# Scores copied to SBUF by VectorE, and transpositions in row halves for two heads, in an attention and two-expert kernel

## The chip, the cores and the metric

The kernel runs on 1 core of one Trainium2 chip. The metric is the device time of one execution in microseconds (us); lower is better. The engines are named as the profile names them: PE is TensorE (PEld its weight loads), DVE is VectorE, ACT is ScalarE, POOL is GpSimd, SP is SyncE, which issues most DMAs.

## The reference

Attention over 2 batches and 8 heads (576 positions of 64), then two expert layers of 1152 x 512 x 2048 x 512, one with the Mish activation, one with a rational function:

```python
q_rot, k_rot = (rotate(q), rotate(k))
scores = scale * np.matmul(q_rot, k_rot.transpose(0, 1, 3, 2))
scores = scores - np.max(scores, axis=-1, keepdims=True)
attn = np.exp(scores)
attn = attn / (np.sum(attn, axis=-1, keepdims=True) + 1e-09)
attn_out = np.matmul(attn, v)
...
h = x @ w_in;  g = h * np.tanh(softplus(h));  x = g @ w_out
h = x @ w_in;  g = P(h) / (Q(h) + 1e-6);      out = g @ w_out
```

## The kernel before, in words

**The attention part** goes over 8 pairs of heads (`NPR`; 2 batches x 4). Of each pair the 576 queries are 4 tiles of 128 rows for each of the two heads, and a last tile (t = 4) that holds the remaining 64 rows of both. For a pair the program issues, each as an operation of a plan:

- `rope.1` to `rope.4` (POOL, for the first pair also DVE) rotate q and k; `turn` (L579, PE) transposes them tile by tile into one PSUM bank; `turn.hi` (L591, ACT) rounds the result, times 0.125 for q, to fp32r in SBUF, and `turn.lo` (L597, L599, DVE) stores what the rounding left.
- `score` (L626, PE): 12 matmuls for the two heads of a tile. Each head uses 64 rows of the array, so that the two can run beside each other; the last tile uses all 128 rows and 6 matmuls. A head's tile takes two of the eight PSUM banks.
- `score.max` (L640, DVE) reduces the scores to their negated maximum; `score.exp` (L644, ACT) reads the scores from PSUM and writes the exponentials to SBUF, with their sum.
- `p.turn` (PE): for a tile and one head four transpositions of 128 x 128 (L681) into one bank, and for two tiles together the rest columns; the last tile's ten transpositions are already halves of 64 rows (L672 to L675). `p.move` (L694, ACT) and `p.move2` (L698, DVE) take turns at copying the bank to SBUF.
- `weigh` (L727, PE) multiplies with v, in two column ranges (256 and 320); `weigh.move` (L732, ACT) copies the result.
- `sum.inv` (L747, L748, DVE) inverts the sums, `sum.turn` (L763, PE) transposes them, `sum.row` and `sum.lo` (L765 ACT, L767 DVE) split them, `sum.spread` (L753, L755, PE) spreads them over the partitions, `x.scale` (L760, DVE) multiplies; `x.hi` and `x.lo` (L771, L773, POOL) split the result.

**The expert part** has two layers, four chunks of 512 hidden columns each, three blocks of 384 tokens: `up` (L886) 48 matmuls, the activation on ACT and DVE, `down` (L970). Weights come as 64-bit words; `prepare` loads half a chunk (1 MB, L390) and rebuilds it with `w.size` (L404, ACT), `w.bound` (L419), `w.shift` (L422), `w.low` (L425) on DVE, `w.hi` (L435, ACT) and `w.lo` (L439, DVE). The four halves of the first chunk are prepared during the attention, through one buffer, so that each load waits until the half before it has been read; the second chunk's buffers lie over memory of the attention.

**What sets the order.** `Plan.op` only records an operation with a cost; `Plan.emit` places them by a list schedule. It takes the operation that could start first (plus a `YIELD` for its name), ties by rank, which is the place in the program plus `EARLY_LATE` for its name; a change of an operation's `form` on PE (all 128 rows, halves of rows, halves of columns) costs 95 ns there, and PSUM banks are given out in the same pass. So each engine's queue is a fixed list that the plan wrote, and each engine works it off in order.

Of the kernel before, what the change touches and what calls it, by code (L numbers as in the profile page):

```python
# [7 lines left out]
F32 = mybir.dt.float32  # L8
# [36 lines left out]
def pool(n, wide=False):  # L45
# [13 lines left out]
    "down": 6381, "down.0": 651, "down.add": -4660, "down.add.0": -371, "g.hi": -1666, "g.hi.0": 8818, "g.lo":  # L59
    2324, "g.low": -4168, "g.low.0": -2960, "load": -4036, "mish": -591, "mish.0": 818, "p.move": -5661,  # L60
    "p.move2": -499, "p.turn": -2139, "ratio.1": 3382, "ratio.10": -1773, "ratio.11": -229, "ratio.2": -62,
    "ratio.3": 1635, "ratio.4": -866, "ratio.5": -3076, "ratio.6": -9113, "ratio.7": -2268, "ratio.9": 3319,
    "rope.1": 6275, "rope.3": 3669, "score": 36, "score.exp": -2880, "start": 868, "store": -567, "sum.inv": 4264,
    "sum.lo": -1016, "sum.row": 11927, "sum.spread": 164, "sum.turn": -1062, "turn": -2960, "turn.hi": 4495,
    "turn.lo": 3138, "up": 645, "up.0": -548, "w.bound": 596, "w.bound.0": 530, "w.hi": 478, "w.hi.0": -4430,
    "w.keep": 262, "w.lo.0": -2459, "w.load": 7247, "w.load.0": 427, "w.low": 168, "w.low.0": 321, "w.shift":
    -187, "w.shift.0": 1322, "w.size": 9168, "w.size.0": 129, "weigh": -325, "weigh.move": 200, "x.hi": -2880,
    "y.hi": -2684, "y.lo": 5352}
# [4 lines left out]
    "down.add": 555, "g.hi": 2, "g.hi.0": 640, "g.lo": 641, "g.low.0": 400, "mish": 1313, "mish.0": 616, "p.move":  # L73
    207, "p.move2": 534, "p.turn": 269, "ratio.10": 67, "ratio.5": 52, "ratio.6": 18, "ratio.8": 170, "ratio.9":
    475, "rope.1": 270, "score.exp": 125, "score.max": 433, "start": 205, "store": 572, "sum.inv": 814, "turn":
    321, "turn.lo": 638, "up.0": 1444, "w.bound": 72, "w.bound.0": 568, "w.hi": 116, "w.hi.0": 287, "w.keep":
    1276, "w.lo": 54, "w.lo.0": 1414, "w.load": 2261, "w.load.0": 559, "w.low.0": 702, "w.shift": 143,
    "w.shift.0": 471, "w.size": 690, "w.size.0": 1181, "weigh": 545, "weigh.move": 548, "x.scale": 189, "y.hi":
    160}
# [177 lines left out]
def block_kernel(ctx: ExitStack, tc: tile.TileContext, q, k, v, w1_in, w1_out, w2_in, w2_out,  # L257
# [205 lines left out]
    ROPE_T = ("tab",)  # L463
# [61 lines left out]
    def turned_first(x, b1, b2, engine):  # L525
# [16 lines left out]
    def turned(p, n, engine, ts=slice(0, 5), at=None):  # L542
# [14 lines left out]
        plan.op("rope.1", engine, cost(128 * m), lambda: eng.tensor_tensor(m1, t4, c, ALU.mult), r=[*src, ROPE_T], w=k1)  # L557
        plan.op("rope.2", engine, cost(128 * m), lambda: eng.tensor_tensor(m2, t4, s, ALU.mult), r=[*src, ROPE_T], w=k2)
# [5 lines left out]
    def columns(p, u, ts=slice(0, 4)):  # L564


        P = Banks(1)
# [9 lines left out]
        def pe():  # L577
            for n, (x, i) in enumerate(rows):
                nc.tensor.transpose(bank(P)[:, n * 128:(n + 1) * 128], view(x.off + 128 * i, 128), idf)  # L579

        def moves():
            x = bank(P)
            if u == "q":
                return [(qT[:, :, c], x[:, 0:m], 0.125)]
            if u == "k":
                return [(kT[:, :, c], x[:, 0:m], 1.0)]
            return [(qT[:, :, 512:640], x[:, 0:128], 0.125)] * (u == "e") + [(kT[:, :, 512:S], x[:, m - 64:m], 1.0)]

        def hi():
            for o, i, f in moves():  # L590
                nc.scalar.mul(o[:, 0], i, f)  # L591

        def lo():
            for o, i, f in moves():
                h = o[:, 0].bitcast(F32)
                if f == 1.0:
                    nc.vector.tensor_tensor(o[:, 1], i, h, ALU.subtract)  # L597
                else:
                    nc.vector.scalar_tensor_tensor(o[:, 1], i, f, h, ALU.mult, ALU.subtract)  # L599
# [6 lines left out]
        plan.op("turn", "PE", 110 * len(rows), pe, r=src + [("idf",)], w=[(P,)])  # L606
# [3 lines left out]
    def score(p, t):  # L610
# [19 lines left out]
        plan.op("score", "PE", 6 * 130 + 15, pe, r=src, w=[(P,) for P in Ps], form="rows" if t < 4 else "all")  # L630
# [25 lines left out]
    def turn_p(p, a, t):  # L656

# [411 lines left out]
```

## Time and profile before

| | |
|---|---|
| time before, median of 3 runs | 561.43 us (561.18 to 561.87) |
| profiled execution: span from first to last instruction | 559.8 us |
| the profiled execution's own time | not listed apart from its span; the runs' median lies 1.63 us above the span |
| busy: PE, DVE, ACT, POOL | 537.8, 453.3, 355.4, 95.8 us |
| attention on PE (first transposition pair to the closed run of `up`) | 10.15 to 161.80 us |
| experts on PE | 161.80 to 555.85 us |

A busy time is the union of an engine's instructions; the mean of one instruction holds a tail that the next one overlaps, so the pace of a queue is read from start to start in the timeline. Idle time is only worth something on the engine that the others wait for.

### The profile page before, as it was taken

What the parts mean: (1) busy time and instruction counts of PE and PEld (TensorE: products, weight loads), DVE (VectorE), ACT (ScalarE), POOL (GpSimd) and SP (SyncE); (2) the same over time, 40 slices, a digit from 0 to 9 for tenths busy, and PEclk for the clock granted to TensorE, in tenths of its full rate; (3) what the DMA queues carried; (4) which work ended last, traced back from release to release, by engine and by line L of the source; (5) the groups of instructions that cost most, each with busy time, mean ns of one, the idle gap of its engine ahead of it and who ended that gap; (6) DMA issues with size and microseconds to landing.
All of it is one profiled execution on the core that took longest, in us unless ns stands there. A gap on an engine that the chain in (4) does not pass through costs nothing.

```text
span 559.8 us, 8739 instructions
## 1 busy us (share of the span) xinstructions
PE 537.8 (96%) x3416; PEld 487.5 (87%) x3416; DVE 453.3 (81%) x618; ACT 355.4 (63%) x540; POOL 95.8 (17%) x100
## 2 busy tenths in 40 slices
PE   3999999999999999999999999999999999999997
PEld 2776777677699999999999999998999988899985
DVE  4777878898938798875999882869999999999982
ACT  1767676687748566837666845658476766776540
POOL 6989878211110000000000000000000000000000
PEclk9999999999999999999999999999999999999999
DMA  5253122311453958382879414044005301200012
GB/s 152 68 151 70 42 62 49 92 49 58 148 170 142 366 199 328 141 309 87 319 273 348 173 81 151 0 151 150 2 1 171 130 1 54 97 2 0 1 70 100
DMA packets 38681, 69.35 MB, mean 124 GB/s; under 512 B 22000, under 2 KB 24560, under 8 KB 37104
## 3 DMA queue, kind: packets, MB, share of 16 engines
q1 hardware_dynamic: 37824, 68.50, 35.2%
q8 instruction: 27, 0.44, 0.3%
q10 hardware_dynamic: 816, 0.30, 0.2%
q14 instruction: 14, 0.11, 0.1%
HBM read 53.84 MB, written 14.94 MB: 123 GB/s over the span
## 4 chain that ended last, share of the span: by engine, by line
PE 91%; DVE 4%; ACT 3%; DMA 1%; issue 1%; SPq 0%; ACTq 0%; DVEq 0%
PE banks L886 36%; PE banks L970 35%; PE banks L681 6%; PE banks L727 6%; PE banks L626 6%; ACT f L644 2%; DVE f L640 2%; PE banks L579 1%; PE banks L753 1%; DMA x<-in_k 1%; DVE f L747 1%; DVE f L422 0%; DVE f L531 0%; PE banks L755 0%; PE banks L672 0%
## 5 line engine op out<-in xcount | busy, mean ns | idle before, releaser
L886 PE MATMUL banks<-r 128*128 128x384 f32 x1152 | 203.7, 335 | 0.0
L970 PE MATMUL banks<-r 128*128 128x384 f32 (+1 forms) x1008 | 201.6, 358 | 0.0
L886 PEld LDWEIGHTS banks<-r 128*128 128x128 f32 x1152 | 200.3, 188 | 0.7
L970 PEld LDWEIGHTS banks<-r 128*128 128x128 f32 x1008 | 180.9, 188 | 16.5
L644 ACT ACTIVATE f<-banks,f 128x576 f32<-128x576 f32 x72 | 52.9, 741 | 23.4 <-DVE f L640 23.1
L640 DVE TENSOR_REDUCE f<-banks 128x1 f32<-128x576 f32 x72 | 51.2, 752 | 16.6 <-PE banks L626 15.9
L976 DVE TENSOR_TENSOR x<-banks,x 128x384 f32<-128x384 f32 (+1 forms) x63 | 35.9, 608 | 11.6 <-PE banks L970 11.6
L626 PE MATMUL banks<-r 64*128 64x288 f32 (+1 forms) x432 | 42.5, 315 | 0.5 <-ACT r L591 0.5
L681 PE MATMUL banks<-f 128*128 128x128 f32 x288 | 40.5, 281 | 2.0 <-ACT f L644 1.9
L727 PE MATMUL banks<-x,f 128*64 128x256 f32 (+1 forms) x320 | 42.4, 411 | 0.0
L912 DVE TENSOR_TENSOR r<-f,r 128x768 fp32r<-128x768 f32 x24 | 22.5, 954 | 24.0 <-ACT f L908 15.9
L626 PEld LDWEIGHTS banks<-r 64*128 64x128 f32 (+1 forms) x432 | 34.6, 192 | 7.0 <-issue 3.5
L681 PEld LDWEIGHTS banks<-f 128*128 128x128 f32 x288 | 32.0, 142 | 7.8 <-ACT f L644 3.9
L908 ACT ACTIVATE r<-banks 128x768 fp32r<-128x768 f32 x24 | 19.4, 813 | 30.2 <-PE banks L886 30.2
L934 ACT ACTIVATE f<-banks,f 128x768 f32<-128x768 f32 x24 | 23.4, 987 | 19.5 <-DVE r L897 14.1
L727 PEld LDWEIGHTS banks<-x,f 128*64 128x64 f32 x320 | 22.1, 136 | 14.5 <-issue 1.4
L938 ACT ACTIVATE f<-f 128x768 f32<-128x768 f32 x24 | 22.5, 938 | 15.2 <-DVE f L933 14.6
L936 DVE TENSOR_TENSOR f<-f,banks 128x768 f32<-128x768 f32 x24 | 22.7, 954 | 11.2 <-ACT f L928 7.0
L896 ACT CAST r<-f 128x768 fp32r<-128x768 f32 x24 | 19.9, 830 | 15.8 <-DVE f L944 15.6
L698 DVE COPY x<-banks 128x512 f32<-128x512 f32 (+2 forms) x52 | 28.6, 572 | 1.2 <-PE banks L681 0.9
L931 ACT ACTIVATE f<-f 128x768 f32<-128x768 f32 x24 | 24.7, 1029 | 6.0 <-DVE f L944 5.6
L694 ACT COPY x<-banks 128x512 f32<-128x512 f32 (+2 forms) x52 | 24.4, 500 | 2.8 <-PE banks L681 2.4
(83 smaller groups left out, 661.8 us busy)
## 6 DMA issues: line engine op xcount, KB each, us to landing
f<-in_moe_w_in SPq DMA_DIRECT2D x16, 1024.0 KB, 6.0
f<-in_moe_w_out SPq DMA_DIRECT2D x16, 1024.0 KB, 6.5
outside<-f SPq DMA_DIRECT2D x12, 1024.0 KB, 4.0
r<-outside SPq DMA_DIRECT2D x12, 1024.0 KB, 6.0
out<-x SPq DMA_DIRECT2D x8, 256.0 KB, 2.4
x<-in_k SPq DMA_DIRECT2D x15, 128.0 KB, 2.8
f<-in_q SPq DMA_DIRECT2D x8, 128.0 KB, 3.2
f<-in_v SPq DMA_DIRECT2D x8, 128.0 KB, 2.4
```

Source lines behind the costliest of these rows:

```text
L626: nc.tensor.matmul(bank(Ps[h])[:, hf, 0:HW], qT[r, x, t * 128:(t + 1) * 128], kT[r, y, hf * HW:(hf + 1) * HW], start=(n == 0), stop=(n == 2))
L640: nc.vector.tensor_reduce(nm, bank(P)[:, :, 0:HW], axis=AX.XY, op=ALU.max, negate=True)
L644: nc.scalar.activation(view(at, 2, HW), bank(P)[:, :, 0:HW], AF.Exp, bias=nm, accum_out=sm)
L681: nc.tensor.transpose(bank(P)[:, (i + n) * 128:(i + n + 1) * 128], x[:, f:f + 128], idf)
L694: nc.scalar.copy(o, i)
L698: nc.vector.tensor_copy(o, i)
L727: nc.tensor.matmul(bank(P)[64 * a:64 * a + 64, 0:n], l, r, start=(kb == 0), stop=(kb == 4), skip_group_check=True)
L886: nc.tensor.matmul(bank(P)[:, i, 0:BW], y[:, cb, f], x[:, cb, tok], start=(cb == 0 and n == 0), stop=(cb == CB - 1 and n == 2))
L931: plan.op("ratio.2", "ACT", act(N, False, 2), lambda: nc.scalar.activation(q_, a, AF.Identity, bias=prm[:, 4:5], scale=prm[:, 5:6]), r=[(b ...
L934: plan.op("ratio.4", "ACT", act(N, True, 2), lambda: nc.scalar.activation(t, h(), AF.Identity, bias=prm[:, 2:3], scale=prm[:, 3:4]), r=[(P ...
L970: nc.tensor.matmul(bank(P)[:, 0:n], x, y, start=(f == 0 and j == 0), stop=(f == FT - 1 and j == 2))
L976: nc.vector.tensor_tensor(total(), bank(P)[:, 0:n], total(), ALU.add)
```

## The change

VectorE no longer only reduces the scores. One instruction multiplies them by -0.125, writes them to SBUF, where the exponentials will stand, and keeps their minimum; the exponential reads SBUF, in place, with scale -1. The factor 0.125 leaves the q columns. The PSUM banks of a tile are free once VectorE is done. Transpositions of q, k, exponentials and sums are done as two halves of 64 rows, the halves in two banks; one `p.turn` does both heads of a tile (16 halves in place of 8 whole ones), and its two moves take one half each, of both heads. `sum.inv` writes its first step to PSUM. All plan costs around this, `EARLY_LATE` and `YIELD` are new, so the order is new on every engine.

```diff
-    return 200.0 if a == "PE" else 80.0 if a == "POOL" else 157.0 if b == "POOL" else 145.0 if a == "ACT" else 118.0
+    return 250.0 if a == "PE" else 80.0 if a == "POOL" else 157.0 if b == "POOL" else 145.0 if a == "ACT" else 118.0
...
+    HALVES = slice(0, 64), slice(64, 128)
...
-        P = Banks(1)
+        P = Banks(2)
...
-                nc.tensor.transpose(bank(P)[:, n * 128:(n + 1) * 128], view(x.off + 128 * i, 128), idf)
+                for hf, r in enumerate(HALVES[:1 if x is xk and i == 4 else 2]):
+                    nc.tensor.transpose(bank(P)[:, hf, n * 64:(n + 1) * 64], view(x.off + 128 * i, 128)[r], idf[r, r])
...
-        plan.op("turn", "PE", 110 * len(rows), pe, r=src + [("idf",)], w=[(P,)])
+        plan.op("turn", "PE", 60 * len(rows) + 20, pe, r=src + [("idf",)], w=[(P,)], form="rows")
...
-            nc.vector.tensor_reduce(nm, bank(P)[:, :, 0:HW], axis=AX.XY, op=ALU.max, negate=True)
+            nc.vector.tensor_scalar(view(at, 2, HW), bank(P)[:, :, 0:HW], -0.125, None, ALU.mult, ALU.min, accum_out=nm)
...
-            nc.scalar.activation(view(at, 2, HW), bank(P)[:, :, 0:HW], AF.Exp, bias=nm, accum_out=sm)
-
-        plan.op("score.max", "DVE", dve(576, True), most, r=[(P,)], w=[(T["nm", p], i)])
-        plan.op("score.exp", "ACT", act(576, True, 2), exp, r=[(P,), (T["nm", p], i)], w=[(e, h), (T["sm", p], i)], form="exp")
+            nc.scalar.activation(view(at, S), view(at, S), AF.Exp, bias=nm, scale=-1.0, accum_out=sm)
+
+        plan.op("score.max", "DVE", dve(576, True) + 90, most, r=[(P,)], w=[(T["nm", p], i), (e, h)])
+        plan.op("score.exp", "ACT", act(576, False, 2), exp, r=[(T["nm", p], i)], w=[(e, h), (T["sm", p], i)], form="exp")
...
-                k = [512] if a is None else [(S + 64) * a + kb * 128 for kb in range(4)]
+                k = [512] if what == "r" else [(S + 64) * a + kb * 128 for a in range(2) for kb in range(4)]
                 for n, f in enumerate(k):
-                    nc.tensor.transpose(bank(P)[:, (i + n) * 128:(i + n + 1) * 128], x[:, f:f + 128], idf)
...
+                    for hf, r in enumerate(HALVES):
+                        nc.tensor.transpose(bank(P)[:, hf, (i + n) * 64:(i + n + 1) * 64], x[r, f:f + 128], idf[r, r])
...
-            nc.vector.tensor_scalar_add(sm, sm, 1e-9)
-            nc.vector.reciprocal(sm, sm)
+            nc.vector.tensor_scalar_add(bank(P)[:, 0, 64:73], sm, 1e-9)
+            nc.vector.reciprocal(sm, bank(P)[:, 0, 64:73])
```

Where the queues stand otherwise than before, at the two places that matter most. First PE's queue in one of the later pairs (L626, after the change L628, is `score`; L681, then L683, `p.turn`; L727, then L732, `weigh`; L753 and L755, then L765 and L767, `sum.spread`). Before:

```order
L626 MATMUL banks<-r 128x288 x24
L753 MATMUL banks<-r 128x128 x4
L755 MATMUL banks<-r 128x64 x2
L681 MATMUL banks<-f 128x128 x18
L626 MATMUL banks<-r 128x288 x18
L681 MATMUL banks<-f 128x128 x8
L727 MATMUL banks<-x,f 64x320 x10
```

With the change:

```order
L628 MATMUL banks<-r 128x288 x36
L683 MATMUL banks<-f 128x64 x16
L732 MATMUL banks<-x,f 64x256 x10
L683 MATMUL banks<-f 128x64 x20
L765 MATMUL banks<-r 128x128 x4
L767 MATMUL banks<-r 128x64 x2
L628 MATMUL banks<-r 128x288 x12
```

The scores of three tiles now stand in a row ahead of the first transposition, and the transpositions come as groups of 16 and 20 halves. Over the whole attention the forms of the matmuls in PE's queue (all rows, row halves, column halves) change 48 times in place of 80.

Second, VectorE's queue at the end of the attention. L760 (after: L772) is the last `x.scale`; L419, L422, L425, L439 (after: L420, L423, L426, L440) are the preparation of a half chunk; L912 (L923) belongs to the first expert block. Before:

```order
L422 TENSOR_SCALAR f<-f 128x1024
L747 TENSOR_SCALAR f<-f 128x9
L748 RECIPROCAL f<-f 128x9
L425 SCALAR_TENSOR_TENSOR f<-f 128x1024
L767 TENSOR_TENSOR r<-banks,r 9x128
L698 COPY x<-banks 128x4x128
L698 COPY x<-banks 128x256
L439 TENSOR_TENSOR r<-f,r 128x1024
L912 TENSOR_TENSOR r<-f,r 128x768
L760 TENSOR_TENSOR f<-f,banks 128x576
```

With the change:

```order
L423 TENSOR_SCALAR f<-f 128x1024
L698 COPY x<-banks 128x8x64
L779 TENSOR_TENSOR r<-banks,r 9x128
L698 COPY x<-banks 128x2x2x64
L426 SCALAR_TENSOR_TENSOR f<-f 128x1024
L440 TENSOR_TENSOR r<-f,r 128x1024
L772 TENSOR_TENSOR f<-f,banks 128x576
L420 TENSOR_SCALAR f<-f 128x1024
L423 TENSOR_SCALAR f<-f 128x1024
L426 SCALAR_TENSOR_TENSOR f<-f 128x1024
L440 TENSOR_TENSOR r<-f,r 128x1024
```

The last half of the first chunk (`down`'s second half) is now prepared behind the last `x.scale`, where before all four halves were ready ahead of it.

## Rows read from the trace of the kernel before

**Rows 1.** The chain that ended last, in order of time (start us, us, what), its end.
```profile
by line: PE banks L886 35.7%; PE banks L970 35.4%; PE banks L681 5.9%; PE banks L727 5.7%; PE banks L626 5.5%; ACT f L644 2.1%; DVE f L640 1.5%; PE banks L579 1.2%; PE banks L753 0.9%; DMA x<-in_k 0.8%; issue 0.6%; DVE f L747 0.6%; DVE f L4
...
161.80 12.57 PE banks L886 x72
174.37 8.32 PE banks L970 x48
...
555.85 0.69 DVE x L976
```
**Rows 2.** Busy time by stretch: stretch, length, PE, PEld, DVE, ACT, POOL, clock, DMA.
```profile
0.00:10.15 10.15, 1.59 (x6) 0.90 (x6) 4.05 (x14) 1.68 (x3) 5.08 (x21) 1.00 0.57 154
10.15:161.80 151.65, 142.20 (x1276) 110.22 (x1277) 119.77 (x204) 106.88 (x263) 88.17 (x77) 1.00 0.31 83
161.80:555.85 394.05, 394.01 (x2137) 376.42 (x2135) 328.82 (x399) 246.85 (x275) 2.58 (x2) 1.00 0.37 139
10.15:28.00 17.85, 16.12 (x129) 13.10 (x130) 12.26 (x21) 11.81 (x32) 17.20 (x19) 1.00 0.37 85
101.00:118.00 17.00, 16.00 (x156) 12.45 (x154) 14.94 (x27) 12.89 (x33) 3.77 (x4) 1.00 0.27 81
118.00:134.00 16.00, 15.03 (x146) 11.49 (x146) 14.20 (x26) 12.82 (x31) 2.58 (x2) 1.00 0.25 85
134.00:154.50 20.50, 19.74 (x180) 14.42 (x179) 18.82 (x33) 14.64 (x37) 2.55 (x2) 1.00 0.31 104
```
**Rows 3.** PE's timeline, transpositions of both kinds (start us, us, what).
```profile
75.02 2.19 PE L681 MATMUL banks<-f 128*128 128x128 f32 x18
76.96 2.02 PE L626 MATMUL banks<-r 128*128 128x288 f32 x18
...
79.93 0.46 PE L672 MATMUL banks<-f 64*128 64x64 f32 x8
80.23 0.22 PE L674 MATMUL banks<-f 64*64 64x64 f32 x1
```
**Rows 4.** PE's timeline, a `score` ahead of either form.
```profile
93.45 1.05 PE L626 MATMUL banks<-r 64*128 64x288 f32 x12
94.44 0.67 PE L753 MATMUL banks<-r 128*128 128x128 f32 x4
...
104.97 1.06 PE L626 MATMUL banks<-r 64*128 64x288 f32 x12
105.86 0.41 PE L672 MATMUL banks<-f 64*128 64x64 f32 x8
```
**Rows 5.** Groups of VectorE by form in the attention, x count, busy us, mean ns.
```profile
L640 DVE TENSOR_REDUCE f<-banks 128x1 f32<-128x576 f32 x72 | 51.2, 752 | 16.6 <-PE banks L626 15.9
L698 DVE COPY x<-banks 128x512 f32<-128x512 f32 x36 | 24.3, 685 | 1.1 <-PE banks L681 0.9
L760 DVE TENSOR_TENSOR f<-f,banks 128x576 f32<-128x576 f32 x7 | 5.3, 754 | 0.4 <-PE banks L755 0.3
L439 DVE TENSOR_TENSOR r<-f,r 128x1024 fp32r<-128x1024 f32 x4 | 4.8, 1209 | 0.4 <-ACT r L435 0.4
L425 DVE SCALAR_TENSOR_TENSOR f<-f 128x1024 int32<-128x1024 int32 x4 | 4.7, 1180 | 0.0
L747 DVE TENSOR_SCALAR f<-f 128x9 f32<-128x9 f32 x8 | 4.5, 561 | 1.8 <-ACT f L644 1.8
L419 DVE TENSOR_SCALAR f<-f 128x1024 f32<-128x1024 f32 x4 | 2.7, 672 | 0.0
```
**Rows 6.** VectorE's line L747: duration ns min/median/max, first and last start.
```profile
L747 DVE TENSOR_SCALAR f<-f x8: 163/338/1482, 25.3 to 152.4; 128x9 f32<-128x9 f32 x8
```
**Rows 7.** ScalarE's timeline, two exponentials in a row.
```profile
111.27 0.73 ACT L644 ACTIVATE f<-banks,f 128x576 f32<-128x576 f32 x1
111.89 0.20 ACT L644 ACTIVATION_READ_ACCUMULATOR f<-banks,f 128x1 f32 x1
111.98 0.74 ACT L644 ACTIVATE f<-banks,f 128x576 f32<-128x576 f32 x1
```
**Rows 8.** Page, groups of ScalarE: the same function read from PSUM and from SBUF.
```profile
L934 ACT ACTIVATE f<-banks,f 128x768 f32<-128x768 f32 x24 | 23.4, 987 | 19.5 <-DVE r L897 14.1 <-PE banks L886 5.4
L931 ACT ACTIVATE f<-f 128x768 f32<-128x768 f32 x24 | 24.7, 1029 | 6.0 <-DVE f L944 5.6
```
**Rows 9.** Who waited for whom in the attention: us in total, times, longest.
```profile
ACT f L644 <- DVE f L640: 23.1, 23, 2.7
DVE f L640 <- PE banks L626: 15.9, 18, 2.5
```
**Rows 10.** Page, DMA issues: KB each, median us from issue to landing.
```profile
f<-in_moe_w_out SPq DMA_DIRECT2D x16, 1024.0 KB, 6.5
```

More of the change, by code (lines that the diff above doesn't have):

```diff
@@ L58 @@
 EARLY_LATE = {
[L59 to L68, printed above, removed]
-YIELD = {
[L73 to L79, printed above, removed]
+    "down": 8105, "down.0": -10238, "down.add": -4500, "down.add.0": 9176, "g.hi": -3468, "g.hi.0": -513, "g.lo":
@@ new lines @@
+    -6844, "g.low": 2705, "g.low.0": -1500, "load": -12, "mish": 2638, "mish.0": -9439, "p.move": 3251, "p.move2":
[3 rows of a table added]
+    6950, "start": -15033, "store": -23613, "sum.inv": 6789, "sum.lo": -1504, "sum.row": -2245, "sum.spread": 12666,
+    "sum.turn": 2209, "turn": 1681, "turn.hi": 81, "turn.lo": -1931, "up": -2977, "up.0": 4642, "w.bound": -664,
+    "w.bound.0": -2122, "w.hi": -3055, "w.hi.0": 1055, "w.keep": 155, "w.lo": 3167, "w.lo.0": 6469, "w.load": 2704,
+    "w.load.0": 1067, "w.low": -2390, "w.low.0": 6407, "w.shift": -2873, "w.shift.0": -5558, "w.size": -5571,
@@ new lines @@
+    "w.size.0": -6628, "weigh": 12363, "weigh.move": 346, "x.hi": 4580, "x.lo": 11809, "x.scale": 4441, "y.hi":
+    -7189, "y.lo": -1086}
+YIELD = {
+    "down": 59, "g.hi.0": 1011, "g.lo": 35, "g.low.0": 2754, "load": 1375, "mish": 710, "mish.0": 137, "p.move":
+    1250, "p.move2": 734, "p.turn": 427, "ratio.11": 757, "ratio.2": 115, "ratio.5": 26, "ratio.9": 422, "rope.1":
+    1107, "rope.2": 1256, "score": 657, "score.exp": 1681, "score.max": 810, "start": 1539, "store": 27, "sum.inv":
+    12, "sum.row": 851, "sum.spread": 609, "sum.turn": 325, "turn": 735, "turn.hi": 1365, "turn.lo": 20, "up": 12,
+    "up.0": 2642, "w.bound": 381, "w.bound.0": 1089, "w.hi.0": 1541, "w.keep": 103, "w.lo": 242, "w.lo.0": 1263,
+    "w.load": 46, "w.load.0": 105, "w.low": 128, "w.low.0": 1254, "w.shift.0": 1166, "w.size": 1770, "w.size.0":
+    2190, "weigh": 1507, "weigh.move": 1060, "x.hi": 271, "x.lo": 1171, "x.scale": 683, "y.lo": 99}
@@ L629, in score @@
         src = [(bq, t // 2 if t < 4 else "e", z) for z in "hl"] + [(bk, u, z) for u in "ke" for z in "hl"]
-        plan.op("score", "PE", 6 * 130 + 15, pe, r=src, w=[(P,) for P in Ps], form="rows" if t < 4 else "all")
+        plan.op("score", "PE", 895 if t < 4 else 880, pe, r=src, w=[(P,) for P in Ps], form="rows" if t < 4 else "all")
         e = T["P", p, t] = plan.ring("P", PR, 2 * S, 3)
@@ L701, in turn_p @@
[L701 to L709 removed]
+            if what == "r":
+                return [(PTr[:, c].rearrange("p (n h j) -> p h n j", h=2, j=64),
+                         x[:, :, 0:m * 64].rearrange("p h (n j) -> p h n j", j=64))]
@@ new lines, in moves, with move @@
+            d = slice(c.start + 64 * hf, c.start + 64 * hf + 64)
+            return [(PTm[:, :, :, d].rearrange("p a k m -> p (a k) m"), x[:, hf, :].rearrange("p (k m) -> p k m", m=64))]
+        def move(engine, hf):
+            for o, i in moves(hf):
+                (nc.scalar.copy if engine == "ACT" else nc.vector.tensor_copy)(o, i)
+        r = [(e, h) for e in es for h in ((0,) if t == 4 else (0, 1))]
+        n = 256 if what == "r" else 512 if t < 4 else 1000
+        plan.op("p.turn", "PE", 140 if what == "r" else 500 if t < 4 else 330, pe, r=r + [("idf",)], w=[(P,)], form="rows")
@@ new lines, in turn_p @@
+        for hf in range(2 if what == "m" and t < 4 else 1):
+            if what == "r":
+                w = blocks("r", c)
+            elif t < 4:
+                w = [k for h in (0, 1) for k in blocks(h, slice(c.start + 64 * hf, c.start + 64 * hf + 64))]
+            else:
+                w = [k for h in (0, 1, "r") for k in blocks(h, c)]
+            T["moves"] = T.get("moves", 0) + 1
+            if T["moves"] % 2:
+                plan.op("p.move", "ACT", act(n), lambda hf=hf: move("ACT", hf), r=[(P,)], w=w)
+            else:
+                plan.op("p.move2", "DVE", dve(n, True) + (0 if n < 600 else 60), lambda hf=hf: move("DVE", hf), r=[(P,)], w=w)
@@ L746, in rec, with turn, row @@
         def rec():
-            nc.vector.tensor_scalar_add(sm, sm, 1e-9)
-            nc.vector.reciprocal(sm, sm)
+            nc.vector.tensor_scalar_add(bank(P)[:, 0, 64:73], sm, 1e-9)
+            nc.vector.reciprocal(sm, bank(P)[:, 0, 64:73])
+        def turn():
+            for hf, h in enumerate(HALVES):
+                nc.tensor.transpose(bank(P)[0:9, hf, 0:64], sm[h], idf[h, h])
+        def row(x):
+            return x.rearrange("p (h j) -> p h j", h=2)
         def spread():
@@ L840, in attention @@
                 at += LAG - 0.5
[L841 to L842 removed]
+                add(at, turn_p, p, "m", t)
                 if t == 1 or t == 3:
[L844 removed]
+                    add(at + 1.1, turn_p, p, "r", t - 1)
             add(g + LAG + 4.2 + (not late), weigh, p, 0)
```

89 lines of the change are left out of this document (32 added, 57 removed), and 3 rows, old and new, of the table EARLY_LATE.

## The prediction

> **What bounds the kernel now.** I read the chain that ended last first [rows 1]: 36% and 35% of it are the two expert lines on PE, and from 161.80 us on it never leaves PE until the last addition. The table by stretch says the same from the other side [rows 2]: in the 394.05 us of the experts PE is busy 394.01, so that nothing the change does to the experts' order can make them shorter, and only a PE that is made to wait could make them longer. The edit has to pay in the attention, between PE's first full run at 10.15 and 161.80. There PE is busy 142.20 of 151.65 us: it is the bound, with 9.45 us idle. VectorE is busy 119.77 (79%), ScalarE 106.88 (70%), POOL 88.17 (58%). But in the last three stretches VectorE is at 14.94 of 17.00, 14.20 of 16.00 and 18.82 of 20.50, 0.88 to 0.92 [rows 2]: behind PE stands a second engine with little room. The waits show the loop between the three [rows 9]: ScalarE waited 23.1 us for the maximum on VectorE, VectorE 15.9 us for scores on PE.
>
> **Transpositions on PE.** Eighteen whole ones take 76.96 - 75.02 = 1.94 us from start to start, 0.108 each; with their share of the pieces between, 0.11 [rows 3]. The halves that the kernel already has for the last tile take 80.23 - 79.93 = 0.30 us for eight, 0.0375 each [rows 3], and the new ones are the same instruction, alternating between the two halves of the array. So:
> - `p.turn`: 256 whole (28.2 us) become 512 halves (19.2): 9.0 less
> - rest columns: 32 (3.5) become 64 (2.4): 1.1 less
> - q and k: 80 (8.8) become 152 (5.7), as k's last tile needs one half: 3.1 less
> - sums: 8 (0.9) become 16 (0.6): 0.3 less
>
> together 13.5 us. **Changes of form:** a `score` is followed after 0.99 us by a matmul over all rows and after 0.89 by a half [rows 4], so a change costs 0.09 to 0.10; 80 less 48 changes times 0.09 is 2.9 us. `weigh`, `score` and `sum.spread` stream the same columns; at nothing. PE's work falls by 16.4, from 142.20 to 125.8 us. With the 9.45 us idle as it was, PE would end the attention at 10.15 + 125.8 + 9.45 = 145.4 instead of 161.80.
>
> **VectorE.** L640 takes 752 ns for 576 elements from PSUM, an elementwise multiplication from PSUM of the same size (L760) 754 [rows 5]: reading and writing 576 costs what reading alone does. What the kept minimum adds no row of VectorE shows. It may add nothing, as for the reduction, which also ends in one column; above stands ScalarE, which fetches its sum with an instruction of its own: 0.20 us long, of which 0.09 delays the next exponential (111.89 to 111.98) [rows 7]. I take 0.09, the delay and not the tail, since VectorE's instructions overlap likewise: 72 x 0.09 = 6.5 us more, with ends 0 and 14.4. The Trainium skill ("VectorE: DVE Perf Modes", section on two Vector instructions with no wait between them) speaks against the change here: an op that also writes out its accumulator counts as two instructions. By it the trace should show a second VectorE row per score; the sum stays at 6.5, and no run here shows it yet.
>
> On the other side `sum.inv` becomes cheap. L747, on nine columns, has a mean of 561 ns, a minimum of 163 and a maximum of 1482 [rows 5, 6]; its long ones lie in the first 100 us, where POOL works. Written to PSUM it should take 0.17 each: 4.5 - 1.4 = 3.1 us less. And the last half chunk is prepared behind `x.scale`: 0.67 + 0.69 (L422 is as long as its undisturbed neighbour L419 within 0.02) + 1.18 + 1.21 = 3.75 us leave the stretch [rows 5]. That step needs cover: its load, 6.5 us to landing [rows 10], is queued on SP behind a load of the second expert's weights that waits for PE and POOL, then come ScalarE, VectorE, ScalarE, VectorE, some 6 us; `down` needs it 12.6 us after the closed run of `up` starts (174.37 less 161.80) [rows 1]. The buffer is free one preparation earlier, so I cost it at nothing; if the load were late by more than about 4 us, PE would wait. VectorE's work in the attention: 119.77 + 6.5 - 3.1 - 3.75 = 119.4 us, as much as before in a shorter stretch.
>
> **ScalarE.** The same function on 768 elements takes 1029 ns from SBUF and 987 from PSUM [rows 8]: 72 x 0.042 = 3.0 us more on an engine that idles 45 us; nothing on the path. In return a tile's two banks come free about 0.7 us sooner, one exponential [rows 7], while the two-head transposition now holds two banks at once; I cost the two together at nothing, with the idle of PE between half and all of the old 9.45 as ends.
>
> **The sum.** PE could end at 145.4, VectorE sets the other limit. In the first 17.85 us it was busy 12.26 [rows 2], waiting for first data, and I keep that. The other 119.4 - 12.26 = 107.1 us go at a busy share that must be chosen: 0.79 is the old mean, 0.918 the best stretch. PE no longer covers for it, so I take 0.879, the lowest of the three late stretches, in which PE was still the slower one: 107.1 / 0.879 = 121.9. The end comes at 28.0 + 121.9 = 149.9, 11.9 us before 161.80. The experts and the tail follow unchanged: span 559.8 - 11.9 = 547.9, and with the 1.63 us around it **549.5 us**, 2.1% under the median of 561.43.
>
> **Rivals.**
> - *PE stays the bound.* If the new order keeps VectorE at 0.918 from 28.0 on, VectorE ends at 144.7 and PE's 145.4 holds: 561.43 - 16.4 = 545.0; with half of PE's idle gone as well, 540.3. For it: the scores of three tiles in a row give VectorE six tiles of work while PE transposes. Against it: six tiles want twelve banks, and there are eight, so that the third score waits for VectorE.
> - *Little room.* At a share of 0.82 VectorE ends at 158.6: 558.2. At the old 0.79 it ends at 163.6, and nothing is gained. For it: three engines at 0.8 and above, each in a fixed order, and VectorE now waits for the buffer of exponentials too, since it writes there, with copies for PE queued behind it.
> - *Slower: the copying minimum is held up by POOL.* L747, a tensor-scalar from SBUF to SBUF, took 0.39 us more than its quick ones of about 0.17, on the mean of eight [rows 5, 6]. If writing the scores to SBUF meets the same obstacle, 72 x 0.39 = 28.1 us come on top: at 0.918 the end is 28.0 + 135.2 / 0.918 = 175.3, that is 574.9 us. It decides from 0.145 us over my price (72 x 0.145 / 0.879 = 11.9), at a mean of about 0.99 us per instruction. Against it: L698 also writes 512 floats from PSUM to SBUF beside POOL and stays at 685 ns [rows 5].
> - *Slower: the clock falls.* The granted clock is 1.00, the 2.4 GHz level, in every stretch, in the first 10.15 us too, when PE worked for 1.59 [rows 2]; a PE that idles more could lose it. At 1.2 GHz each us of work costs one more, so 12 of the 125.8 us at the lower level eat the gain, and a quarter gives 549.5 + 31.5 = 581. The Trainium skill's page "TensorE: Matmul & The Clock Gate", in its part on the transposition, holds that transpositions do not count as activity that engages the full clock; by that rule more than here would have to be slow already, and the trace disagrees: 1.00 in stretches where a third of PE's instructions are transpositions.
>
> **How the numbers follow.** VectorE limits near the forecast (546 to 555): 0.50. PE stays the bound (540 to 546): 0.25. Little room (555 to 560): 0.12. No change: 0.04. POOL holds up VectorE: 0.05; the clock: 0.02; another wait, a late weight load for instance: 0.02. Faster by more than 0.2%, which is 1.1 us and about what a measurement here can tell from none: 0.87; within it 0.04; slower 0.09. The range goes from 541 (PE's limit with about half its idle gone) to 558 (a share of 0.82); outside it are the slow cases, no change, and a little at either end.
>
> **What would show it.** Right: the closed run of `up` starts near 150; the halves stay at 0.0375 us and PE's busy time ahead of it near 126; VectorE is busy at 0.85 or more from 28 us on; the new L642 costs 0.75 to 0.85 us, L752 about 0.17; clock 1.00; PE full from there to the end. Wrong: L642 near 1 us or more, halves that take turns at 0.055 or more (then the transpositions cost what they did), PE idle inside the experts, or VectorE idle a fifth of the time with PE waiting for it at the `score`.

## The result, and the profile after

The changed kernel takes 546.12 us (median of 4 runs, 545.62 to 546.84) beside 561.3 us for the kernel before on the same chip; the ratio is 0.9736, with a 95% interval of 0.9718 to 0.9754. That is 15.2 us less, where 11.9 were forecast; the time lies inside the range of 541 to 558. The profiled execution took 546.36 us, with a span of 544.6.

The head of the page with the change (busy us, share of the span, instructions):

```profile
span 544.6 us, 9576 instructions
...
PE 523.9 (96%) x3784; PEld 477.5 (88%) x3784; DVE 452.3 (83%) x690; ACT 359.1 (66%) x544; POOL 98.0 (18%) x100
```

PE's busy time was 537.8 us before, so it fell by 13.9; its idle time fell from 559.8 - 537.8 = 22.0 to 20.7 us. The gain is nearly all PE work, and PE is as full as it was.

The table by stretch, same columns as [rows 2], for the attention, the attention from 28 us on, and the experts:

```profile
10.15:146.47 136.32, 128.75 (x1640) 100.26 (x1640) 113.53 (x272) 107.37 (x262) 88.48 (x74) 1.00 0.31 85
28.00:146.47 118.47, 113.36 (x1453) 86.69 (x1452) 100.83 (x240) 93.75 (x226) 71.76 (x58) 1.00 0.30 85
146.47:540.50 394.03, 394.03 (x2136) 376.54 (x2136) 333.67 (x404) 250.09 (x281) 3.10 (x2) 1.00 0.38 142
```

Beside [rows 2] the experts are as long as before (394.03 and 394.05 us), and the closed run of `up` starts at 146.47 where it started at 161.80. Of these 15.33 us PE's work gave 142.20 - 128.75 = 13.45, its idle time 9.45 - 7.57 = 1.88. From 28 us on PE is busy 113.36 of 118.47 us (96%), VectorE 100.83 (85%): PE is still the fullest engine.

VectorE's groups with the change (count, busy us, mean ns, idle before):

```profile
L642 DVE TENSOR_SCALAR_CACHE_REDUCE f<-banks 128x576 f32<-128x576 f32 x72 | 51.8, 754 | 4.2 <-PE banks L628 2.9 <-ACT x L698 0.3 <-issue 0.2
L642 DVE DVE_READ_ACCUMULATOR f<-banks 128x1 f32 x72 | 6.0, 84 | 0.0
L752 DVE TENSOR_SCALAR banks<-f 128x9 f32<-128x9 f32 x8 | 1.3, 167 | 3.5 <-ACT f L646 3.4
```

The copying minimum answers to the reduction in [rows 5] (752 ns), and L752 to L747 (561 ns). The minimum now has a second row of 84 ns. What that row costs shows in VectorE's timeline (start us, us, what):

```profile
29.15 0.76 DVE L642 TENSOR_SCALAR_CACHE_REDUCE f<-banks 128x576 f32<-128x576 f32 x1
29.83 0.08 DVE L642 DVE_READ_ACCUMULATOR f<-banks 128x1 f32 x1
29.83 0.75 DVE L642 TENSOR_SCALAR_CACHE_REDUCE f<-banks 128x576 f32<-128x576 f32 x1
30.51 0.08 DVE L642 DVE_READ_ACCUMULATOR f<-banks 128x1 f32 x1
30.51 0.75 DVE L642 TENSOR_SCALAR_CACHE_REDUCE f<-banks 128x576 f32<-128x576 f32 x1
```

From start to start two of them stand 0.68 us apart. The next instruction begins at the same time as the read of the accumulator, so the extra row lies beside it. In the kernel before the instruction behind a reduction starts 0.66 us after it:

```profile
19.56 0.75 DVE L640 TENSOR_REDUCE f<-banks 128x1 f32<-128x576 f32 x1
20.22 0.68 DVE L698 COPY x<-banks 128x512 f32<-128x512 f32 x1
```

So the kept minimum costs 0.01 to 0.02 us, not the 0.09 of the forecast.

The waits with the change (us in total, times, longest), which answer to [rows 9]:

```profile
ACT f L646 <- DVE f L642: 12.1, 10, 2.7
PEld banks L628 <- DVE f L642: 4.3, 12, 0.5
DVE f L642 <- PE banks L628: 2.9, 5, 1.4
PE banks L628 <- DVE f L642: 1.9, 7, 0.3
```

VectorE hardly waits for scores any more (2.9 us, from 15.9), and ScalarE waits half as long for the minimum (12.1, from 23.1). In their place PE's `score` waits for VectorE to free banks, briefly and often. The place is PE's timeline at the third score of a row:

```profile
128.56 1.06 PE L628 MATMUL banks<-r 64*128 64x288 f32 x11 [0.28 <-DVE f L642]
129.33 0.79 PE L683 MATMUL banks<-f 64*128 64x64 f32 x16
130.05 2.38 PE L732 MATMUL banks<-x,f 128*64 128x256 f32 x20
132.36 0.84 PE L683 MATMUL banks<-f 64*128 64x64 f32 x20
133.01 0.64 PE L765 MATMUL banks<-r 64*128 64x128 f32 x4
```

Three tiles in a row ask for twelve banks, and eight are there: a score is cut into pieces by a wait of 0.28 us. Behind it sixteen halves take 130.05 - 129.33 = 0.72 us with the change of form, twenty take 0.65.

### The profile page after: what moved, and what is told of

The parts are those of the page before. It is cut to its first block, busy times and chain, and to the rows that moved or that the text cites. A ratio compares the mean times of both kernels' runs of the same rounds, so it can differ in the third digit from the quotient of the medians.

```text
span 544.6 us, 9576 instructions
## 1 busy us (share of the span) xinstructions
PE 523.9 (96%) x3784; PEld 477.5 (88%) x3784; DVE 452.3 (83%) x690; ACT 359.1 (66%) x544; POOL 98.0 (18%) x100
## 4 chain that ended last, share of the span: by engine, by line
PE 90%; DVE 4%; ACT 3%; issue 2%; DMA 1%; SPq 0%; DVEq 0%; ACTq 0%
PE banks L897 37%; PE banks L981 36%; PE banks L732 7%; PE banks L628 5%; PE banks L683 3%; DVE f L642 1%; ACT f L646 1%; DVE x L698 1%; DVE r L601 1%; DMA x<-in_k 1%; PE banks L765 1%; ACT r L597 1%; ACT x L698 0%; DVE f L533 0%; PE banks L582 0%
## 5 line engine op out<-in xcount | busy, mean ns | idle before, releaser
L646 ACT ACTIVATE f<-f 128x576 f32<-128x576 f32 x72 | 55.5, 773 | 12.4 <-DVE f L642 12.1
L642 DVE TENSOR_SCALAR_CACHE_REDUCE f<-banks 128x576 f32<-128x576 f32 x72 | 51.8, 754 | 4.2 <-PE banks L628 2.9
L628 PE MATMUL banks<-r 64*128 64x288 f32 (+1 forms) x432 | 48.6, 324 | 4.5 <-DVE f L642 1.9
L987 DVE TENSOR_TENSOR x<-banks,x 128x384 f32<-128x384 f32 (+1 forms) x63 | 38.5, 611 | 14.5 <-PE banks L981 14.4
L628 PEld LDWEIGHTS banks<-r 64*128 64x128 f32 (+1 forms) x432 | 38.4, 196 | 10.4 <-DVE f L642 4.3
L732 PE MATMUL banks<-x,f 128*64 128x256 f32 (+1 forms) x320 | 42.5, 410 | 0.6 <-DVE r L601 0.3
L923 DVE TENSOR_TENSOR r<-f,r 128x768 fp32r<-128x768 f32 x24 | 22.9, 957 | 17.6 <-ACT f L919 17.5
L732 PEld LDWEIGHTS banks<-x,f 128*64 128x64 f32 x320 | 23.4, 136 | 13.6 <-issue 0.7
L919 ACT ACTIVATE r<-banks 128x768 fp32r<-128x768 f32 x24 | 19.6, 815 | 17.0 <-PE banks L897 16.8
L939 ACT ACTIVATE f<-banks 128x768 f32<-128x768 f32 x24 | 19.4, 807 | 16.9 <-PE banks L897 14.7
L949 ACT ACTIVATE f<-f 128x768 f32<-128x768 f32 x24 | 22.2, 937 | 9.8 <-DVE f L944 9.6
L683 PEld LDWEIGHTS banks<-f 64*128 64x128 f32 x576 | 22.7, 144 | 5.6 <-issue 2.8
L908 DVE TENSOR_TENSOR r<-f,r 128x768 fp32r<-128x768 f32 x24 | 22.7, 957 | 4.2 <-ACT r L907 3.7
L683 PE MATMUL banks<-f 64*128 64x64 f32 x576 | 25.5, 231 | 0.7 <-ACT f L646 0.3
```

What stands on the lines that cost most here:

```text
L628: nc.tensor.matmul(bank(Ps[h])[:, hf, 0:HW], qT[r, x, t * 128:(t + 1) * 128], kT[r, y, hf * HW:(hf + 1) * HW], start=(n == 0), stop=(n == 2))
L642: nc.vector.tensor_scalar(view(at, 2, HW), bank(P)[:, :, 0:HW], -0.125, None, ALU.mult, ALU.min, accum_out=nm)
L646: nc.scalar.activation(view(at, S), view(at, S), AF.Exp, bias=nm, scale=-1.0, accum_out=sm)
L683: nc.tensor.transpose(bank(P)[:, hf, (i + n) * 64:(i + n + 1) * 64], x[r, f:f + 128], idf[r, r])
L732: nc.tensor.matmul(bank(P)[64 * a:64 * a + 64, 0:n], l, r, start=(kb == 0), stop=(kb == 4), skip_group_check=True)
L908: plan.op("g.lo", "DVE", dve(N), lambda: nc.vector.tensor_tensor(gl, g, gh.bitcast(F32), ALU.subtract), r=[(x,), (dst, u, "h")], w=[(dst, ...
```

## The experiments

Two theories stood after the result. **PE theory:** the attention ends when PE's work is done, and the halves (less work on PE) are the gain. **Order theory:** the three engines are all nearly full, and the gain comes from the two new rank tables, the banks that come free sooner, or both; the halves only take part.

### The halves undone, with the order of the change

`e1_whole` makes the transpositions of q, k, exponentials and rest columns whole again and leaves the plan's costs and so every queue's order as it is; in the traces VectorE, ScalarE and POOL work in the order of the change. Its two moves per tile still take one half of the columns each, and so both read both banks. The edit for the exponentials:

```diff
-                    for hf, r in enumerate(HALVES):
-                        nc.tensor.transpose(bank(P)[:, hf, (i + n) * 64:(i + n + 1) * 64], x[r, f:f + 128], idf[r, r])
+                    nc.tensor.transpose(bank(P)[:, (i + n) // 4, (i + n) % 4 * 128:(i + n) % 4 * 128 + 128], x[:, f:f + 128], idf)
...
-            return [(PTm[:, :, :, d].rearrange("p a k m -> p (a k) m"), x[:, hf, :].rearrange("p (k m) -> p k m", m=64))]
+            return [(PTm[:, :, :, d], x.rearrange("p a (k h m) -> p a k h m", k=4, h=2)[:, :, :, hf, :])]
```

> The order of every queue is that of the changed kernel, row for row; only the transpositions of q, k, exponentials and rest columns are whole ones over 128 rows again (0.11 us each by the trace of before, in place of two halves of 0.0375), in the same two banks, and the moves read the same number of elements. PE gets 368 whole ones for 728 halves: 40.5 less 27.3 is 13.2 us more work, and some 30 changes of form at 0.09, together about 16 us. Theory A (VectorE sets the pace, PE idles 7.6 us in the attention): part of it is hidden, 8 to 12 us slower, about 555 us. Theory B (PE is still the bound): the whole 16 us, about 562 us. Theory C (the gain came from banks that come free earlier and from the new order, not from the halves): under 5 us, below 551 us.

Measured: 566.4 us, ratio to the kernel before 1.0089 (1.0067 to 1.011), 20.3 us over the change and more than any of the three theories allowed. But from 28 us on ScalarE's moves waited 23.9 us in 28 waits for VectorE's, which they do not in the changed kernel; the experiment had added a wait of its own. `e5_whole_head` gives each move one head, and so one bank:

```diff
-            return [(PTm[:, :, :, d], x.rearrange("p a (k h m) -> p a k h m", k=4, h=2)[:, :, :, hf, :])]
+            return [(PTm[:, hf, :, c], x[:, hf, :].rearrange("p (k m) -> p k m", k=4))]
...
-                w = [k for h in (0, 1) for k in blocks(h, slice(c.start + 64 * hf, c.start + 64 * hf + 64))]
+                w = blocks(hf, c)
```

> As the run with whole transpositions, in the same order of every queue, but each of the two moves takes one head, and so one bank, where there both moves read both banks and ScalarE waited 23.9 us for VectorE. PE's extra work is the same, VectorE and ScalarE copy as many elements. Theory B (PE is the bound, and the work of the whole transpositions is the loss): 562 to 566 us, at most 4 us less than there. Theory D (the loss there came mostly from the two moves taking turns at the banks): 552 to 557 us.

Measured: 561.21 us (10 runs), ratio 1.0 (0.9985 to 1.0015), 15.1 us over the change and just below the 562 to 566 of theory B. Its attention in the table by stretch:

```profile
10.15:159.75 149.60, 145.79 (x1285) 110.41 (x1284) 115.20 (x272) 108.35 (x262) 88.53 (x74) 1.00 0.28 78
```

With the queues held, PE's work rises by 145.79 - 128.75 = 17.0 us and its idle time falls from 7.57 to 3.81; VectorE and ScalarE do as much as with the change, within 1.7 us. So of the 17.0 us of work 159.75 - 146.47 = 13.3 reach the end of the attention in the two profiled executions, 0.78 of it; the medians lie 15.1 apart. In this order the halves are worth the whole gain, and most of their work reaches the time: the PE theory holds, though not one for one.

### One engine more loaded, with the order of the change

Three kernels add work to one engine each. `e2_dve_plus`: 144 copies of seven columns on VectorE; as they read a tile's banks, these also come free a little later. `e3_pe_plus`: 256 more halves, 9.6 us by the price of 0.0375. `e4_act_plus`: 72 copies of one column on ScalarE.

```diff
+            for n in range(2):
+                nc.vector.tensor_copy(tiny[:, 2 + 7 * n:9 + 7 * n], bank(P)[:, n, 0:7])
...
+                if what == "m":
+                    for n, f in enumerate(k[:4]):
+                        for hf, r in enumerate(HALVES):
+                            nc.tensor.transpose(bank(P)[:, hf, n * 64:(n + 1) * 64], x[r, f:f + 128], idf[r, r])
...
+            nc.scalar.copy(prm[:, 8 + i % 8:9 + i % 8], nm)
```

> Same order on every queue; behind each of the 72 copies with minimum VectorE copies seven columns from each of the tile's two banks to a scratch place, which nothing reads: 144 short instructions, by the nearest row (an accumulator read of 0.084 us) some 0.08 us each, 11 us in all, if none overlaps. Theory A (VectorE sets the pace): the time grows by 8 to 11 us, at least 0.7 us per us added. Theory B (PE is the bound): below 0.3 us per us, under 3.5 us. Theory C (a loop of waits, no engine alone): about half.

> Same order on every queue; each two-head transposition of a tile first does eight of its sixteen halves once more, into the place that the later ones overwrite: 32 x 8 x 0.0375 = 9.6 us more on PE. Theory A (VectorE sets the pace): under 0.4 us per us added, below 4 us. Theory B (PE is the bound): 0.8 to 1, 8 to 9.6 us. Theory C (a loop of waits): about half.

> Same order on every queue; behind each of the 72 exponentials ScalarE copies one column to a place that nothing reads: some 0.1 to 0.2 us each, 7 to 14 us in all. ScalarE is busy 79% of the attention. Theories A and B: hidden, under 0.2 us per us added. Theory C (a loop of waits through maximum and exponential): a third to a half, 3 to 6 us.

Measured: VectorE's dose 551.01 us, ratio 0.9829 (0.9802 to 0.9857), +4.9 over the change; PE's 553.3, the median of three, ratio 0.9854 (0.9834 to 0.9875), +7.2; ScalarE's 547.65, ratio 0.9755 (0.974 to 0.977), +1.5. One of the four executions of PE's dose took 1829.63 us and is left out. It was the profiled one: in its trace PE is busy for 1812.6 us, 48 matmuls of an expert block take 29.6 us where the change takes 8.32, and there is no record of the clock; why is open. The attention with VectorE's dose, then with ScalarE's:

```profile
10.15:150.55 140.40, 129.83 (x1640) 99.61 (x1640) 124.00 (x416) 108.45 (x262) 88.40 (x74) 1.00 0.30 83
```

```profile
10.15:147.66 137.51, 129.41 (x1646) 100.77 (x1642) 113.97 (x273) 112.66 (x334) 88.54 (x74) 1.00 0.31 85
```

VectorE's work rose by 124.00 - 113.53 = 10.47 us and the time by 4.9: 0.47 us per us (0.39 by the attention of the profiled executions, which grew by 140.40 - 136.32 = 4.08). ScalarE's rose by 5.29 and the time by 1.5: 0.28 (0.22 by the attention, 1.19 longer). For PE it is 7.2 / 9.6 = 0.75, with a dose that stands by its price alone. No engine is the limit alone and none is free; PE counts most. That is theory C for VectorE, a little under theory B for PE, and between the two for ScalarE.

### The old ranks, and the copy or the halves with the order they then get

`e8_old_ranks` is the changed kernel with `EARLY_LATE` and `YIELD` of the kernel before. `e6_copy_only` is the kernel before with the copying minimum alone and its own old tables. `e7_halves_only` is the changed kernel with the maximum and the exponentials on PSUM again, and the new tables; it leaves out the factor 0.125 on the scores, which is assumed to cost no time. In all three the plan is written anew, so the order moves on every engine.

```diff
 EARLY_LATE = {
-    "down": 8105, "down.0": -10238, "down.add": -4500, "down.add.0": 9176, "g.hi": -3468, "g.hi.0": -513, "g.lo":
...
+    "down": 6381, "down.0": 651, "down.add": -4660, "down.add.0": -371, "g.hi": -1666, "g.hi.0": 8818, "g.lo":
...
-            nc.vector.tensor_scalar(view(at, 2, HW), bank(P)[:, :, 0:HW], -0.125, None, ALU.mult, ALU.min, accum_out=nm)
+            nc.vector.tensor_reduce(nm, bank(P)[:, :, 0:HW], axis=AX.XY, op=ALU.max, negate=True)
...
-            nc.scalar.activation(view(at, S), view(at, S), AF.Exp, bias=nm, scale=-1.0, accum_out=sm)
+            nc.scalar.activation(view(at, 2, HW), bank(P)[:, :, 0:HW], AF.Exp, bias=nm, accum_out=sm)
```

The first piece is e8's, the others are e7's; e6 makes them the other way round, with the factor -1 in place of -0.125.

> The changed kernel with the tables of ranks and yields of before. Everything else, the costs too, is as after the change. If the order is of little account beside the work (theory B alone): 546 to 549 us. If the ranks had to be fitted to the new costs (theory E): 551 us or more, with PE idle longer than 7.6 us in the attention and its busy time the same.

> The kernel before, with one part of the change alone: VectorE copies the scores (times -1, as q keeps its factor) with their minimum, the exponential reads SBUF; whole transpositions, all other plan costs and the ranks of before (the plan places anew). PE's work stays. Theory B (PE is the bound): under 3 us gained, 558 to 561 us. Theory C (banks that come free an exponential earlier are what pays): 550 to 556 us.

> The changed kernel with the scores' part undone: VectorE reduces, the exponential reads PSUM (the factor 0.125 is left out, which costs no time); halves, all other costs and the new ranks stay, the plan places anew. PE's work is that of the changed kernel. Theory B (PE's work is the gain): 546 to 550 us. Theory C (the copy to SBUF pays, since banks come free earlier): 552 us or more.

Measured: old ranks 560.06 us (10 runs), ratio 0.9979 (0.9958 to 0.9999); copy alone 564.44, ratio 1.0066 (1.0042 to 1.009); halves alone 576.08, ratio 1.0273 (1.0232 to 1.0314). The attention with the old ranks, then with the halves alone:

```profile
10.15:158.11 147.96, 135.03 (x1640) 104.20 (x1640) 114.73 (x275) 108.37 (x262) 87.63 (x77) 0.97 0.29 79
```

```profile
10.15:169.59 159.44, 136.42 (x1616) 101.44 (x1616) 116.98 (x204) 104.22 (x261) 88.41 (x74) 0.91 0.28 80
```

With the same instructions as the change, the old ranks give 13.9 us of the gain back: PE idles 12.93 us in place of 7.57, and the same matmuls take 135.03 us in place of 128.75, with a mean granted clock of 0.97. So the order theory has its part too, though PE's busy time was expected to stay. But the two kernels with one part alone run in tables that were made for something else, and both took longer than any theory had it. For the copy alone its trace shows what the order cost: the closed run of `up` starts at 158.13 us, 3.67 ahead of the kernel before, but in the first `down` PE then waits 5.18 us, until 177.44, for VectorE's last step on a half chunk of weights (L439), with a clock of 0.50 from 174.6 to 181.4. So 564.44 us is no verdict on the copy. The halves alone let PE idle 159.44 - 136.42 = 23.0 us in the attention, and say little of the halves either.

### Each part with tables of its own

So four kernels got rank tables from one and the same search, for the plan that ends first by the plan's own costs, all with the change's 250 for the way from PE: both parts (`e9_both_fit`), the halves alone, the copy alone, and neither. The first also has the minimum at its measured cost.

```diff
-        plan.op("score.max", "DVE", dve(576, True) + 90, most, r=[(P,)], w=[(T["nm", p], i), (e, h)])
+        plan.op("score.max", "DVE", dve(576, True) + 12, most, r=[(P,)], w=[(T["nm", p], i), (e, h)])
```

> The changed kernel with the planner's cost of the copying minimum lowered from 90 ns over a reduction to 12 ns (the trace showed about 10), and the two rank tables fitted anew to that; every instruction stays, only the order moves. Theory: PE is the bound of the attention, busy 128.75 us of 136.32 with the change, so a better order can take away idle time of PE alone, 7.57 us at the most; no lower than 539, and 542 to 547 expected. Rival (the order on record is one lucky draw, since the old ranks gave 560.06 with the same instructions): another fitted order lands anywhere between 546 and 560.

> The changed kernel without the copy: maximum and exponentials read the banks again (the factor 0.125 on the scores is left out), the transpositions stay in halves, and the ranks are fitted anew to these costs in the same manner as in the run with both. Theory A (the copy matters, since it gives a bank back one exponential, about 0.7 us, sooner, and the two-head transposition needs two banks): PE, with its 128.75 us of work, idles for more than the 7.57 us of the change, and the time is 551 to 558. Theory B (the copy is worth nothing, only the halves and an order that fits): within 1.5 us of the run with both. The 576.08 us with the unfitted order then was the order's fault under either.

> The kernel before with the copy alone: the minimum writes the scores to SBUF and the exponentials read there, transpositions whole, the sums as before, ranks fitted anew in the same manner. PE's work in the attention stays at about 142 us (before: 142.20 of 151.65), so with no idle time at all it would end at 152.4 and the time would be 552.0. Theory A (the banks that come free sooner take away waits of PE): 553 to 557. Theory B (no gain without the halves, as 564.44 with the old order said): 559 to 564.

> The kernel before with its ranks fitted anew in the same manner and nothing else: what the fitting alone is worth. Theory (the parts carry the gain and the old order was already as good as this kernel allows, PE busy 142.20 of 151.65 us): 557 to 563. Rival (the new order carries most of the gain): 548 to 556; no lower than 552.0 as long as PE's work stays at 142.20 us.

| kernel | time, us | ratio to before (95%) | PE busy / idle in the span, us |
|---|---|---|---|
| both, tables of the change | 546.12 | 0.9736 (0.9718 to 0.9754) | 523.9 / 20.7 |
| both, searched | 546.89 | 0.9751 (0.9729 to 0.9772) | 523.9 / 20.8 |
| copy alone, searched | 553.37 | 0.9855 (0.9832 to 0.9878) | 535.7 / 14.1 |
| halves alone, searched | 571.96 | 1.0188 (1.0151 to 1.0225) | 533.9 / 33.5 |
| neither, searched | 568.44 | 1.0129 (1.0112 to 1.0147) | 538.7 / 27.9 |

The attention of the copy alone and of the halves alone, by stretch:

```profile
10.00:147.45 137.45, 134.62 (x1249) 105.15 (x1248) 113.73 (x268) 103.88 (x256) 87.89 (x74) 1.00 0.30 82
```

```profile
10.00:155.47 145.47, 132.96 (x1633) 100.56 (x1632) 112.59 (x197) 104.40 (x260) 87.35 (x74) 0.98 0.29 81
155.47:563.00 407.53, 398.30 (x2136) 378.75 (x2136) 334.04 (x403) 256.92 (x281) 3.08 (x2) 0.99 0.37 137
```

Four things follow. First, a second pair of tables, in which every number is another, gives 546.89, so the order on record is not the only one that does it. As the search began at the first pair, the two are not independent, and the rival of a lucky draw is weakened rather than gone. The plan's wrong cost of 90 ns did no harm that shows; no version here beats the change. Second, the copy alone does gain, 561.3 - 553.37 = 7.9 us, if its order fits; theory B of that run, that it gains nothing without the halves, falls. PE then idles 2.83 of 137.45 us, next to 9.45 of 151.65 before. The stretch itself must not be set beside the others' end, as it ends with 4.2 us more of PE work left for the experts (398.25 us there, PE busy in all of them, where the change has 394.03). Third, the halves without the copy gain nothing that shows: 571.96 beside 568.44, both over the kernel before and over what either of their theories allowed. The factor 0.125 is left out here as in e7. Fourth, part of that is not the attention's: with the halves alone PE also idles 407.53 - 398.30 = 9.2 us among the experts, so this search did worse there. In the attention alone the halves without the copy end 9.0 us later than the change (155.47 to 146.47): 12.51 us idle in place of 7.57, and 132.96 us for the same work in place of 128.75, at a mean clock of 0.98.

How good a table is moves the time by several us: neither part, searched, is 7 us slower than the kernel before with its own table. So what the copy is worth stands between 8 us (beside the kernel before) and 25 (571.96 - 546.89, both searched, with the halves), and no run here held the order while taking the copy away, so its worth in the order of the change is open. The halves, too, are worth less than e5 says once each kernel has tables of its own: beside the copy 553.37 - 546.89 = 6.5 us, where the held order gave 15.1. An order made for whole transpositions takes more than half of their price back.

## Why the prediction was right, and where it failed

The verdict, faster, and the range were right; the likeliest case was not the one that came. Step by step:

- **The bound, and the experts** [rows 1, 2]: right. 394.03 us with PE busy in all of them; all of the gain lies ahead of the closed run.
- **A half at 0.0375 us** [rows 3]: right. With the change, sixteen take 0.72 us with the change of form and twenty 0.65, so 0.03 to 0.045 each. By e5 undoing them adds 17.0 us of PE work, where 13.5 for the transpositions and 2.9 for the changes of form were counted.
- **PE's work at 125.8 us:** it came to 128.75. The missing 3 us stand for the most part at the `score`: from start to start in PE's queue, idle time left out, its matmuls take 42.8 us where they took 40.3 (by busy time, which counts tails, L628 has 48.6 and L626 had 42.5). e5 bears it out: with whole transpositions in the new order PE is busy 145.79 us, 3.6 more than before. Scores are cut into pieces where they wait for banks, as at 128.56; that this is what makes them longer is likely, but no run takes it apart. The wait for banks the first rival had named (twelve banks, eight there); the sum had no term for it.
- **The accumulator's price, 0.09 us, 6.5 in all:** mis-sized. The nearest row was ScalarE's [rows 7], and VectorE does not behave like it: 0.01 to 0.02 us per instruction, about 1 in all, near the lower end of 0. The Trainium skill ("VectorE: DVE Perf Modes", section on two Vector instructions with no wait between them) counts such an instruction as two. The trace agrees as to the rows, 72 of 84 ns each; the page gives no time, and these rows lie beside the next instruction.
- **`sum.inv` at 0.17 us** [rows 6]: right, 0.167 with 158 to 171 ns from first to last, so the long ones beside POOL are gone.
- **The late half chunk** at nothing: right. `down` starts at 159.16, 12.69 us after the closed run of `up`, with no wait on PE.
- **ScalarE at +3.0 us, nothing on the path:** the size was right (55.5 us after 52.9), the price nearly: at 0.28 per us it is 0.7.
- **"VectorE sets the other limit", at a busy share of 0.879:** this is the step of the sum that gave 549.5, and it failed. With the accumulator at 1 us, its own working has 101.6 us in place of 107.1, and 28.0 + 101.6 / 0.879 = 143.6 for VectorE, ahead of PE's 145.4. Then PE is the bound, and the sum says 545.0, the figure of the first rival; 546.12 was measured. That the two lie so close is partly luck: PE had 3 us more work than that sum has, and idled 1.9 us less. And a share is no fixed limit: with e2's dose VectorE ran at 124.00 / 140.40 = 0.88 over the whole attention, start included.
- **The banks, "at nothing", and the order, taken as given:** these two went through without a price, and the gain hangs on them. With the old ranks 13.9 us are lost, and without the copy, in the tables searched for that, 9.0 us in the attention alone.

Of the rivals, *PE stays the bound* came true, with three quarters of PE's work reaching the time. *POOL holds up the minimum* did not: the longest L642 took 759 ns. *Little room* did not either: VectorE ran at 0.85 from 28 us on. *The clock falls* did not happen in the changed kernel's profiled execution (one of the three others has a mean of 0.996, at 545.88 us), but it did in others of these kernels. The prediction's "1.00 in the first 10.15 us too" is a wrong reading: the last section shows PE at about half its pace until 16.8 us. And stretches in which two thirds of PE's instructions are other matmuls cannot speak against the rule on transpositions that it quotes.

## What to carry to other kernels

Where a faster unit of work needs more buffers at once, look at who frees them: here, with the tables that were found, the halves paid only beside the copy that gives PSUM banks back one exponential sooner, and only in an order made for both. When three engines stand above 0.75, a sum of the slowest engine's work is a start, but each engine's work counts in part (here about 0.75, 0.47 and 0.28 per us on PE, VectorE and ScalarE), and a small dose on each in a fixed order measures that directly. To undo one part of a change, hold the order of every queue; an order that is written anew can hide or feign some 14 us.

## What was not expected of the hardware

The granted clock falls within the attention in some of these kernels, most where PE idles most: it is 0.91 with 23.0 us idle in `e7_halves_only` and 0.97 with 12.9 in `e8_old_ranks`. The sum of idle time alone does not set it: `e6_copy_only` has 0.99 with 5.2 us idle by 158.13, the kernel before 1.00 with 9.45. In the halves alone with searched tables it goes like this (5 us stretches, columns as before; then PE's timeline):

```profile
60.00:65.00 5.00, 4.77 (x51) 3.05 (x51) 4.80 (x10) 2.62 (x9) 2.42 (x2) 1.00 0.29 66
65.00:70.00 5.00, 3.83 (x44) 3.04 (x45) 4.87 (x10) 4.65 (x12) 3.37 (x3) 0.98 0.72 239
70.00:75.00 5.00, 4.53 (x41) 4.06 (x39) 3.10 (x6) 2.30 (x6) 5.00 (x5) 0.50 0.49 114
75.00:80.00 5.00, 5.00 (x67) 3.56 (x66) 2.20 (x4) 3.42 (x9) 4.84 (x5) 0.84 0.16 37
```

```profile
67.28 0.66 PE L766 MATMUL banks<-r 64*128 64x128 f32 x4 [0.66 <-ACT f L647]
67.78 0.35 PE L768 MATMUL banks<-r 64*128 64x64 f32 x2
68.00 0.71 PE L684 MATMUL banks<-f 64*128 64x64 f32 x16
68.72 0.33 PE L583 MATMUL banks<-f,x 64*128 64x64 f32 x3
69.08 1.93 PE L629 MATMUL banks<-r 64*128 64x288 f32 x12
```

PE was busy 3.83 of 5 us, and then worked at 0.50, the 1.2 GHz level, for some 6 to 7 us: the twelve matmuls of a score took 1.93 us, where [rows 4] has 1.05. It makes waits on PE dearer than their length: with the old ranks the idle time rose by 5.4 us and the time of the same matmuls by 6.3, of which the mean clock of 0.97 over 147.96 us accounts for 4 to 5 (an estimate). What exactly sets it off no run here tells apart, since before has a stretch of 4 us with PE busy 2.73 at a clock of 1.00.

At the start the column needs care. It shows 1.00 from 0 us on, but the trace's first record of the clock begins at 16.8 us in the kernel before and at 19.3 with the change. Four whole transpositions of the kernel before, ahead of that and later:

```profile
14.86 1.12 PE L681 MATMUL banks<-f 128*128 128x128 f32 x4 [0.27 <-ACT f L644]
15.77 0.85 PE L579 MATMUL banks<-f,x 128*128 128x128 f32 x3
...
60.40 0.66 PE L681 MATMUL banks<-f 128*128 128x128 f32 x4
60.89 0.60 PE L579 MATMUL banks<-f,x 128*128 128x128 f32 x4
```

From start to start the four take 0.91 us early and 0.49 later, nearly half the pace, which fits the 1.2 GHz level. Both kernels begin like this (their first 24 matmuls of a `score` take 3.28 and 3.25 us), so little of the difference between them comes from it.

The other surprise is the accumulator of VectorE, whose read is a row of its own and delays the next instruction by 0.01 to 0.02 us at most, while ScalarE's delays it by 0.09 us [rows 7].
